# A tile of their own for the normalized rows, and a new order for the three products of split matmuls

## The chip, the core and the metric

The kernel runs on one core of a Trainium2 chip. The metric is the device time of one execution in microseconds (us), the median over runs. TensorE does the matmuls (PE in the rows, and PEld for its weight loads), VectorE is DVE, ScalarE is ACT, GpSimd is POOL, and SyncE (SP) issues the DMAs.

## What is computed

Eight batches of 3136 rows of 256 numbers go through a spectral filter and then through an MLP with a Fourier mix. Cut to what matters:

```python
# spectral filter
X = rfft(x, axis=1)
Yr = Xr @ w_r - Xi @ w_i + b_r ;  Yi = Xr @ w_i + Xi @ w_r + b_i
Y = softshrink(Yr, 0.01) + 1j * softshrink(Yi, 0.01)
x = irfft(Y, n=3136, axis=1)
# mix and MLP
u = x + real(fft(fft(x, axis=1), axis=2))
un = (u - mean(u)) / sqrt(var(u) + 1e-6)        # over the 256 numbers of a row
out = u + maximum(un @ w_ch1, 0) @ w_ch2        # 256 -> 1024 -> 256
```

## The kernel before

The Fourier transforms are matmuls against tables: 3136 is split into 64 by 49. Each batch b goes through stages, each of them a Python generator: `p1` (first transform, products into PSUM tile `g_f1`), `p2_f2` (second transform, `g_f2`, which yields X and the sums Xs), `p2_w` (the weights, `g_w`), `p2_mix` (the Fourier mix, `g_mix`, stored in DRAM as `md`), `p2_yt` and `p2_g2` (the way back, `g_yt` and `g_g2`, stored as `bd`), then the MLP in groups of three or four blocks of 128 rows: `p3_norm` loads `bf` and `mt` by DMA, multiplies (`g_g1`), adds `mt`, takes mean and variance and normalizes; `p3_tr` transposes the normalized rows on PE (`g_ut`); `p3_mlp1` multiplies with w1 into `h` and splits the rectified result; `p3_mlp2` multiplies with w2 into `o`, adds the rows and stores them.

To keep precision an operand is split in a high part and a low part (`hh` and `hl`, `uth` and `utl`, `bh` and `bl`, `xh` and `xl`, `Xh` and `Xl`, `yh` and `yl`). ACT makes the high part by a copy into the type fp32r; DVE (`lo_v`, L144, and L738 for `hl`) or POOL (`lo_g`, L147) then makes the low part as the difference. `mm3` multiplies two split operands by three matmuls into the same PSUM region: L150 is high left with low right, L151 low left with high right, L152 high with high. The left one is the stationary operand, for which a weight load goes ahead of every matmul. The operand that has just been made is the left one in `p3_mlp2` (`hh`, `hl`), and the right one in all the others (`p1`, `p2_w`, `p2_g2`, `p3_norm`, `p3_mlp1`), where the left one is a table or a weight.

Every `yield` gives a due time, and a heap runs the generators in that order, which gives the order in which instructions are traced. The tile context is opened with `schedule_with_timeline_sim=True`: a planner then orders the instructions of each engine by its own model of time, and takes a later one that is ready before an earlier one that is not. It also writes the semaphore waits: an instruction carries one, and further ones stand before it as separate EVENT_SEMAPHORE instructions on its queue. All DMAs are issued in order from the one queue of SP.

Tiles with the same tag share that tag's buffers in turn. Tag `mt` (2 KB per partition, 2 buffers) holds the rows loaded from `md` (L673, L675); L683 adds them to `g_g1` into `ut`; then L700 writes the normalized rows into the same `mt`, and L718 transposes them from there. It also holds scratch tiles while the weights are converted (`split_double`, L169 to L189), `wi` and `inv_f`. Tag `im` (0.8 KB, 2 buffers) is scratch in `p2_f2` between a copy on ACT (L445) and an add on DVE (L446), for the pieces that take the second branch: two of four in each quarter of batch 0, one of four in the others.

Of the kernel before, what the change touches and what calls it, by code (L numbers as in the profile page):

```python
# [10 lines left out]
F32 = mybir.dt.float32  # L11
# [117 lines left out]
def spectral_block(ctx: ExitStack, tc: tile.TileContext, x, w_ri, b_ri, w1, w2,  # L129
# [19 lines left out]
    def mm3(o, lh, ll, rh, rl, start=True, stop=True):  # L149
        te.matmul(o, lh, rl, start=start, stop=False)  # L150
        te.matmul(o, ll, rh, start=False, stop=False)  # L151
        return te.matmul(o, lh, rh, start=False, stop=stop)  # L152
# [5 lines left out]
    def split_double(name, h, l, sl, src):  # L158
# [3 lines left out]
        def tmp(tag, bufs, dt=I32):  # L162
            return sb.tile([128, 512], dt, tag=tag, bufs=bufs, name=f"cv_{name}_{tag}")
# [4 lines left out]
        tf = tmp("mt", 2, F32)  # L168
# [10 lines left out]
        r = tmp("mt", 2)  # L179
# [25 lines left out]
    def load_consts():  # L205
# [6 lines left out]
        wi = sb.tile([128, 2, D], F32, tag="mt", bufs=2, name="wi")  # L212
# [17 lines left out]
        inv = sb.tile([128, 128], F32, tag="mt", bufs=2, name="inv_f")  # L230
# [159 lines left out]
    def p2_f2(b):  # L390


        for q in range(4):
# [17 lines left out]
            for ui in range(4):  # L411
# [30 lines left out]
                else:  # L442
                    im = sb.tile([128, 2, 2, S], F32, tag="im", bufs=2, name="im")
# [178 lines left out]
    def p2_g2(b):  # L622

        bd = b_dram[b] = dr.tile([N2, 2, U, D], F32, tag="bd", bufs=4, name=f"bd{b}")
        for q in range(4):
            base, STEP, F2W, W0, WW, M0 = clock2(b, q)
            for i in range(4):
# [4 lines left out]
                for v in range(2):  # L632
                    cols = slice(v * D, v * D + D)
                    t = 2 * (i % 2) + v
                    if b == 0:
                        te.matmul(g[:98, cols], tih[:, t], yh[:, cols], start=True, stop=True)
                    else:
                        mm3(g[:98, cols], tih[:, t], til[:, t], yh[:, cols], yl[:, cols])
# [15 lines left out]
    def p3_norm(b):  # L654

        for gi, (g0, z) in enumerate(groups[b % 2]):
            t0, T3 = clock3(b, g0)
            for i, n in parts_of[z]:
# [8 lines left out]
                mt = sb.tile([128, 2, D], F32, tag="mt", bufs=2, name="mt")  # L667
# [30 lines left out]
                gp.tensor_mul(rs[:, :n], rs[:, :n], vv[:, :n])  # L698
                for j in range(n):
                    va.tensor_scalar(mt[:, j], ut[:, j], ag[:, j, 0:1], rs[:, j], op0=ALU.subtract, op1=ALU.mult)  # L700
                normed[b, gi, i] = mt
                uts[b, gi, i] = ut

    def p3_tr(b):
        for gi, (g0, z) in enumerate(groups[b % 2]):
            t0, T3 = clock3(b, g0)
            for i, n in parts_of[z]:
# [5 lines left out]
                mt = normed.pop((b, gi, i))  # L713
                g = gtile("g_ut")
                gv = g.rearrange("p (k t) -> p k t", k=2)
                for j in range(n):
                    for k in range(2):
                        te.transpose(gv[:, k, j * 128:(j + 1) * 128], mt[:, j, k * 128:(k + 1) * 128], ident)  # L718
# [4 lines left out]
    def p3_mlp1(b):  # L723
        for gi, (g0, z) in enumerate(groups[b % 2]):
            t0, T3 = clock3(b, g0)
            w = z * 128
            for f in range(8):
# [5 lines left out]
                for k in range(2):  # L733
                    mm3(h[:, :w], w1h[:, k, fs], w1l[:, k, fs], uth[:, k, :w], utl[:, k, :w], start=(k == 0), stop=(k == 1))
# [6 lines left out]
    def p3_mlp2(b):  # L741
        for gi, (g0, z) in enumerate(groups[b % 2]):
            t0, T3 = clock3(b, g0)
            for f in range(8):
# [5 lines left out]
                for j in range(z):  # L750
# [3 lines left out]
                        stop=(f == 7 and (j % 2 == 1 or j == z - 1)))  # L754
# [68 lines left out]
```

## Time and profile before

| | us |
|---|---|
| median of 3 runs (1953.55 to 1960.75) | 1956.1 |
| the profiled execution | 1961.45 |
| its span, first to last instruction | 1959.7 |
| around the span | 1.75 |
| PE busy in the span | 1856.2 |
| mean granted TensorE clock | 0.969 of full speed |

A row of a group of instructions names line, engine, operation, out<-in by the tiles' names and how often it ran, then busy time and mean duration, then the idle time of the engine just before them and what ended it. Matmuls overlap in the pipeline, so the distance between two starts, not the duration, is what one costs. Clock 1.00 is 2.4 GHz, and its lower level is 1.2 GHz.

### The profile page before, as it was taken

The page shows a single profiled execution, that of the slowest core. Times are in us where ns is not written, and L with a number is a line of the kernel's source. Part 1 is how long each engine was busy: PE and PEld are TensorE (multiplying, and loading weights), DVE is VectorE, ACT ScalarE, POOL GpSimd, SP SyncE. Part 2 cuts the span into 40 slices and gives each one's busy share as a digit, 9 for nine tenths or more (in the row PEclk, how much of TensorE's full clock was granted, in tenths as well). Part 3 has the DMA queues.
Part 4 walks back from the last instruction along what each step waited for, and adds up shares of the span by engine and source line. Part 5 has one row for each costly group of instructions (what it writes and reads, how often), then busy time and mean ns, then how long its engine had stood idle before and what let it go on. Part 6 is the DMA issues. An engine that isn't in the chain of part 4 may idle for free.

```text
span 1959.7 us, 35047 instructions
## 1 busy us (share of the span) xinstructions
PE 1856.2 (95%) x12115; PEld 1709.1 (87%) x12115; DVE 1322.5 (67%) x2831; ACT 853.2 (44%) x1888; POOL 704.8 (36%) x1087
## 2 busy tenths in 40 slices
PE   4875799999999999999999999999999999999999
PEld 3764699989999999998999999998999998998999
DVE  2676677777776777766677777766777766675543
ACT  2443544444444454443444544434544434433322
POOL 0345544344433444343333443323543322322210
PEclk7886899999999999999999999999999999999999
DMA  7466654345443544434443444435433332223210
GB/s 215 122 177 192 154 139 131 101 119 148 115 122 109 152 129 121 117 98 138 136 134 104 136 137 114 127 99 141 136 106 98 107 98 89 83 70 109 68 41 25
DMA packets 163540, 233.05 MB, mean 119 GB/s; under 512 B 27484, under 2 KB 107428, under 8 KB 163364
## 3 DMA queue, kind: packets, MB, share of 16 engines
q1 hardware_dynamic: 163364, 230.82, 41.9%
q8 instruction: 97, 1.59, 0.3%
q14 instruction: 79, 0.65, 0.1%
HBM read 127.95 MB, written 102.76 MB: 118 GB/s over the span
## 4 chain that ended last, share of the span: by engine, by line
PE 80%; DVE 7%; DMA 6%; SPq 3%; issue 2%; ACT 1%; POOL 1%; DVEq 0%; POOLq 0%; ACTq 0%
PE o L150 8%; PE o L151 8%; PE o L152 8%; PE h L150 8%; PE h L151 8%; PE h L152 8%; PE g_f L419 4%; PE g_w L150 3%; PE g_w L152 3%; PE g_w L151 3%; PE g_g L150 2%; PE g_g L152 2%; PE g_g L151 2%; PE g_yt L609 2%; PE g_ut L718 2%
## 5 line engine op out<-in xcount | busy, mean ns | idle before, releaser
L151 PE MATMUL o<-w2h,hl 128*128 128x256 f32 x1568 | 431.4, 285 | 8.4 <-DVE hl L738 8.4
L738 DVE SCALAR_TENSOR_TENSOR hl<-h,hh 128x512 fp32r<-128x512 f32 (+1 forms) x416 | 272.3, 655 | 243.8 <-ACT hh L737 242.5
L737 ACT ACTIVATE hh<-h 128x512 fp32r<-128x512 f32 (+1 forms) x416 | 238.0, 573 | 443.0 <-PE h L152 382.7
L152 PE MATMUL o<-w2h,hh 128*128 128x256 f32 x1568 | 424.2, 280 | 0.0
L150 PE MATMUL o<-w2l,hh 128*128 128x256 f32 x1568 | 397.6, 286 | 2.5 <-DVE ut L757 2.3
L150 PE MATMUL h<-utl,w1h 128*128 128x512 f32 (+1 forms) x832 | 323.5, 389 | 8.1 <-DVE hl L738 8.1
L152 PE MATMUL h<-uth,w1h 128*128 128x512 f32 (+1 forms) x832 | 317.0, 381 | 0.0
L151 PE MATMUL h<-uth,w1l 128*128 128x512 f32 (+1 forms) x832 | 316.6, 381 | 0.0
L151 PEld LDWEIGHTS o<-w2h,hl 128*128 128x128 f32 x1568 | 297.3, 190 | 14.8 <-DVE hl L738 10.3
L152 PEld LDWEIGHTS o<-w2h,hh 128*128 128x128 f32 x1568 | 297.0, 189 | 3.2
L150 PEld LDWEIGHTS o<-w2l,hh 128*128 128x128 f32 x1568 | 286.3, 189 | 15.1 <-ACT Xsh L428 2.9
L147 POOL TENSOR_TENSOR bl<-bf,bh 128x512 fp32r<-128x512 f32 x104 | 130.0, 1251 | 298.3 <-ACT bh L678 296.1
L419 PE MATMUL g_f<-tff,af 98*128 98x100 f32 x1024 | 155.2, 284 | 25.8 <-DMA tff<-c_tf 13.0
L419 PEld LDWEIGHTS g_f<-tff,af 98*128 98x128 f32 x1024 | 148.5, 204 | 34.2 <-issue 23.4
L152 PEld LDWEIGHTS h<-uth,w1h 128*128 128x128 f32 x832 | 156.8, 189 | 23.8
L150 PEld LDWEIGHTS h<-utl,w1h 128*128 128x128 f32 x832 | 157.0, 189 | 22.8 <-DVE hl L738 9.0
L147 POOL TENSOR_TENSOR xl<-xf,xh 128x512 fp32r<-128x512 f32 (+1 forms) x75 | 97.1, 1295 | 203.2 <-ACT xh L362 201.3
L151 PEld LDWEIGHTS h<-uth,w1l 128*128 128x128 f32 x832 | 157.3, 189 | 13.4
L683 DVE TENSOR_TENSOR ut<-g_g,mt 128x512 f32<-128x512 f32 x104 | 68.3, 657 | 104.9 <-PE g_g L152 67.9
L147 POOL TENSOR_TENSOR Xl<-xx,Xh 128x400 fp32r<-128x400 f32 (+1 forms) x96 | 106.3, 1110 | 89.6 <-ACT Xh L428 69.3
L147 POOL TENSOR_TENSOR Xsl<-xs,Xsh 128x200 fp32r<-128x200 f32 x120 | 76.9, 642 | 161.4 <-ACT Xsh L428 144.2
L700 DVE TENSOR_SCALAR mt<-ut,ag,rs 128x256 f32<-128x256 f32 x196 | 90.8, 502 | 48.9 <-POOL rs L698 48.6
(155 smaller groups left out, 3811.3 us busy)
## 6 DMA issues: line engine op xcount, KB each, us to landing
bd<-bev SPq DMA_DIRECT2D x128, 196.0 KB
af<-ad SPq DMA_DIRECT2D x62, 392.0 KB
bf<-bd SPq DMA_DIRECT2D x184, 128.0 KB
out_dram<-ut SPq DMA_DIRECT2D x92, 256.0 KB
xf<-in_x SPq DMA_DIRECT2D x176, 128.0 KB
ad<-ev SPq DMA_DIRECT2D x168, 128.0 KB
md<-mq SPq DMA_DIRECT2D x112, 192.0 KB
mt<-md SPq DMA_DIRECT2D x416, 32.0 KB
```

Source lines behind the costliest of these rows:

```text
L147: gp.tensor_sub(out_, full, hi.bitcast(F32))
L150: te.matmul(o, lh, rl, start=start, stop=False)
L151: te.matmul(o, ll, rh, start=False, stop=False)
L152: return te.matmul(o, lh, rh, start=False, stop=stop)
L419: te.matmul(g[:, o:o + 100], afs[s][:, ui * D + k * 128:ui * D + k * 128 + 128], tfs[s][:, ui], start=True, stop=True)
L609: te.transpose(gt[:100, (v * 2 + o) * 128:(v * 2 + o + 1) * 128], y[:, o, place].rearrange("p c j -> p (c j)"), ident)
L683: va.tensor_add(ut[:, :n], g[:, :w].rearrange("p (n d) -> p n d", d=D), mt[:, :n])
L700: va.tensor_scalar(mt[:, j], ut[:, j], ag[:, j, 0:1], rs[:, j], op0=ALU.subtract, op1=ALU.mult)
L718: te.transpose(gv[:, k, j * 128:(j + 1) * 128], mt[:, j, k * 128:(k + 1) * 128], ident)
L737: sc.activation(hh[:, :w], h[:, :w], AF.Relu)
L738: va.scalar_tensor_tensor(hl[:, :w], h[:, :w], 0.0, hh[:, :w].bitcast(F32), op0=ALU.max, op1=ALU.subtract)
```

## The change

`mm3` gets a parameter `first` that says which of the three products goes first; the other two follow in the order high·high, high·low, low·high. By default (`p1`, `p2_w`, `p3_norm`) the first is now high·high. In `p2_g2` and `p3_mlp1` it is high left with low right, as before, but the second and third change places. In `p3_mlp2` low left with high right, `hl`·w2h, is first. In all of them two products with the same stationary operand now follow each other. The normalized rows get a tile `nm` of the tag `mt`, which has three buffers instead of two; the tag `im` has one instead of two.

```diff
--- before.py
+++ after.py
@@ -146,10 +146,12 @@
     def lo_g(out_, full, hi):
         gp.tensor_sub(out_, full, hi.bitcast(F32))
 
-    def mm3(o, lh, ll, rh, rl, start=True, stop=True):
-        te.matmul(o, lh, rl, start=start, stop=False)
-        te.matmul(o, ll, rh, start=False, stop=False)
-        return te.matmul(o, lh, rh, start=False, stop=stop)
+    def mm3(o, lh, ll, rh, rl, start=True, stop=True, first=0):
+
+        ops = [(lh, rh), (lh, rl), (ll, rh)]
+        ops.insert(0, ops.pop(first))
+        for i, (l, r) in enumerate(ops):
+            te.matmul(o, l, r, start=start and i == 0, stop=stop and i == 2)
 
     UTB = 6
     st_eng = nc.sync
@@ -165,7 +167,7 @@
         raw = sb.tile([128, 1024], I32, tag="uth", bufs=2, name="raw_" + name)
         behind(1, out=raw.rearrange("p (f e) -> p f e", f=src.shape[1]), in_=src)
         lo, hi = raw[:, 0::2], raw[:, 1::2]
-        tf = tmp("mt", 2, F32)
+        tf = tmp("mt", 3, F32)
         sc.activation(tf, hi.bitcast(F32), AF.Abs)
         va.tensor_scalar(tf, tf, HI_MIN, HI_MAX, op0=ALU.max, op1=ALU.min)
         t = tf.bitcast(I32)
@@ -176,7 +178,7 @@
         wf = w.bitcast(F32)
         e = tmp("ut", UTB)
         va.tensor_scalar(e, w, -0x800000, None, op0=ALU.bitwise_and)
-        r = tmp("mt", 2)
+        r = tmp("mt", 3)
         va.tensor_scalar(r, lo, 8, None, op0=ALU.logical_shift_right)
         rf = tmp("ut", UTB, F32)
         va.scalar_tensor_tensor(rf, r, 2.0 ** -44, e.bitcast(F32), op0=ALU.mult, op1=ALU.mult)
@@ -209,7 +211,7 @@
         for name, tag in (("wr", "hh"), ("ws", "hh"), ("wd", "hl")):
             KF[name] = sb.tile([128, 2, D], F32, tag=tag, bufs=2, name=name + "f")
         behind("x", out=KF["wr"], in_=w_v[0])
-        wi = sb.tile([128, 2, D], F32, tag="mt", bufs=2, name="wi")
+        wi = sb.tile([128, 2, D], F32, tag="mt", bufs=3, name="wi")
         behind("x", out=wi, in_=w_v[1])
 
         for name, sign in (("ws", -1.0), ("wd", 1.0)):
@@ -227,7 +229,7 @@
         sc.copy(cs[:, :, 0], t[:, :, 0:128])
         lo_v(cs[:, :, 1], t[:, :, 0:128], cs[:, :, 0])
         sc.copy(cs[:, 0, 1, 0:1], t[:, 0, 128:129])
-        inv = sb.tile([128, 128], F32, tag="mt", bufs=2, name="inv_f")
+        inv = sb.tile([128, 128], F32, tag="mt", bufs=3, name="inv_f")
         nc.sync.dma_start(out=inv, in_=c_inv)
         split("inv", inv)
 
@@ -440,7 +442,7 @@
                     put(lo_g, [Xl, Xh], xv_)
                     va.tensor_add(xs, xx[:, :, :, 0], xx[:, :, :, 1])
                 else:
-                    im = sb.tile([128, 2, 2, S], F32, tag="im", bufs=2, name="im")
+                    im = sb.tile([128, 2, 2, S], F32, tag="im", bufs=1, name="im")
                     put(sc.copy, [Xh], gv)
                     sc.copy(im, gv[:, :, :, S:])
                     va.tensor_add(xs, gv[:, :, :, :S], im)
@@ -635,7 +637,7 @@
                     if b == 0:
                         te.matmul(g[:98, cols], tih[:, t], yh[:, cols], start=True, stop=True)
                     else:
-                        mm3(g[:98, cols], tih[:, t], til[:, t], yh[:, cols], yl[:, cols])
+                        mm3(g[:98, cols], tih[:, t], til[:, t], yh[:, cols], yl[:, cols], first=1)
                 bev = sb.tile([98, 512], F32, tag="bev", bufs=2, name="bev")
                 (va.tensor_copy if b else sc.copy)(bev, g[:98])
                 u = 8 * q + 2 * i
@@ -664,7 +666,7 @@
 
                 src = [(b - 1, m), (b, m)] if joint else [(b, m), (b, NM + m)]
                 bf = sb.tile([128, 512], F32, tag="bf", bufs=2, name="bf")
-                mt = sb.tile([128, 2, D], F32, tag="mt", bufs=2, name="mt")
+                mt = sb.tile([128, 2, D], F32, tag="mt", bufs=3, name="mt")
                 for r, (bb, n2) in enumerate(src):
                     nc.sync.dma_start(out=bf[r * 64:r * 64 + 64, :w].rearrange("p (n d) -> p n d", d=D),
                                       in_=n2_rows(b_dram[bb], n2, n))
@@ -696,9 +698,10 @@
                 gp.tensor_mul(vv[:, :n], vv[:, :n], rs[:, :n])
                 gp.tensor_scalar(vv[:, :n], vv[:, :n], -0.5, 1.5, op0=ALU.mult, op1=ALU.add)
                 gp.tensor_mul(rs[:, :n], rs[:, :n], vv[:, :n])
+                nm = sb.tile([128, 2, D], F32, tag="mt", bufs=3, name="nm")
                 for j in range(n):
-                    va.tensor_scalar(mt[:, j], ut[:, j], ag[:, j, 0:1], rs[:, j], op0=ALU.subtract, op1=ALU.mult)
-                normed[b, gi, i] = mt
+                    va.tensor_scalar(nm[:, j], ut[:, j], ag[:, j, 0:1], rs[:, j], op0=ALU.subtract, op1=ALU.mult)
+                normed[b, gi, i] = nm
                 uts[b, gi, i] = ut
 
     def p3_tr(b):
@@ -710,12 +713,12 @@
                     uth = sb.tile([128, 2, 512], F32R, tag="uth", bufs=2, name="uth")
                     utl = sb.tile([128, 2, 512], F32R, tag="utl", bufs=2, name="utl")
                     uthl[b, gi] = uth, utl
-                mt = normed.pop((b, gi, i))
+                nm = normed.pop((b, gi, i))
                 g = gtile("g_ut")
                 gv = g.rearrange("p (k t) -> p k t", k=2)
                 for j in range(n):
                     for k in range(2):
-                        te.transpose(gv[:, k, j * 128:(j + 1) * 128], mt[:, j, k * 128:(k + 1) * 128], ident)
+                        te.transpose(gv[:, k, j * 128:(j + 1) * 128], nm[:, j, k * 128:(k + 1) * 128], ident)
                 tw = slice(i * 128, i * 128 + n * 128)
                 sc.copy(uth[:, :, tw], gv[:, :, :n * 128])
                 lo_v(utl[:, :, tw], gv[:, :, :n * 128], uth[:, :, tw])
@@ -731,7 +734,7 @@
                 h = ps.tile([128, 512], F32, tag="h", bufs=2, name="h")
                 fs = slice(f * 128, f * 128 + 128)
                 for k in range(2):
-                    mm3(h[:, :w], w1h[:, k, fs], w1l[:, k, fs], uth[:, k, :w], utl[:, k, :w], start=(k == 0), stop=(k == 1))
+                    mm3(h[:, :w], w1h[:, k, fs], w1l[:, k, fs], uth[:, k, :w], utl[:, k, :w], start=(k == 0), stop=(k == 1), first=1)
                 hh = sb.tile([128, 512], F32R, tag="hh", bufs=2, name="hh")
                 hl = sb.tile([128, 512], F32R, tag="hl", bufs=2, name="hl")
                 sc.activation(hh[:, :w], h[:, :w], AF.Relu)
@@ -751,7 +754,7 @@
                     o = ops[j // 2][:, (j % 2) * D:(j % 2) * D + D]
                     js = slice(j * 128, j * 128 + 128)
                     mm3(o, hh[:, js], hl[:, js], w2h[:, f], w2l[:, f], start=(f == 0 and j % 2 == 0),
-                        stop=(f == 7 and (j % 2 == 1 or j == z - 1)))
+                        stop=(f == 7 and (j % 2 == 1 or j == z - 1)), first=2)
             for (i, n), o in zip(parts_of[z], ops):
                 ut = uts.pop((b, gi, i))
                 va.tensor_add(ut[:, :n], o[:, :n * D].rearrange("p (n d) -> p n d", d=D), ut[:, :n])
```

## Rows read from the trace of the kernel before

**Rows 1.** The page's part 1: the span, then busy time, share of the span and instructions of two engines.
```profile
span 1959.7 us, 35047 instructions
...
PE 1856.2 (95%) x12115; PEld 1709.1 (87%) x12115; DVE 1322.5 (67%) x2831; ACT 853.2 (44%) x1888; POOL 704.8 (36%) x1087
```

**Rows 2.** Busy time by stretch: length, then busy us and number of instructions of PE, PEld, DVE, ACT and POOL, then the granted clock, the busy share of the DMA engines and GB/s.
```profile
0.00:265.00 265.00, 186.35 (x895) 154.08 (x896) 157.38 (x307) 109.14 (x258) 98.03 (x126) 0.80 0.60 168
265.00:1955.00 1690.00, 1669.51 (x11221) 1554.88 (x11220) 1164.14 (x2524) 744.04 (x1632) 606.74 (x961) 1.00 0.40 111
1955.00:1960.00 5.00, 0.30 (x3) 0.10 (x1) 1.02 (x2) 0.00 (x0) 0.00 (x0) 0.71 0.23 80
```

**Rows 3.** What PE waited for from 250 us on, all of it: us in total, times, the longest.
```profile
PE o L151 <- DVE hl L738: 8.4, 10, 2.8
PE h L150 <- DVE hl L738: 8.1, 2, 4.8
PE o L150 <- DVE ut L757: 2.3, 2, 1.4
PE g_ut L718 <- DVE mt L700: 1.2, 3, 0.7
PE g_yt L609 <- DVE ut L683: 0.3, 1, 0.3
```

**Rows 4.** The same for the first 265 us, the longest, and those for POOL's low parts.
```profile
PE g_f L419 <- DMA tff<-c_tf: 13.0, 3, 9.4
PE g_f L419 <- DMA af<-ad: 12.2, 2, 8.5
PE g_ut L718 <- DVE mt L700: 12.0, 1, 12.0
...
PE g_g L150 <- POOL bl L147: 7.3, 1, 7.3
PE g_f L150 <- POOL xl L147: 5.6, 2, 3.2
```

**Rows 5.** Matmuls of PE in order of time, deep in the steady part: start, duration, engine, line, operation.
```profile
1014.43 0.28 PE L150 MATMUL o<-w2l,hh 128*128 128x256 f32 x1
1014.55 0.28 PE L151 MATMUL o<-w2h,hl 128*128 128x256 f32 x1
1014.66 0.28 PE L152 MATMUL o<-w2h,hh 128*128 128x256 f32 x1
1014.77 0.39 PE L150 MATMUL h<-utl,w1h 128*128 128x512 f32 x1
1015.00 0.40 PE L151 MATMUL h<-uth,w1l 128*128 128x512 f32 x1
```

**Rows 6.** First-transform matmuls of batch 0, which all have the same stationary operand, and their weight loads (groups by line: busy us, mean ns, idle before).
```profile
L313 PE MATMUL g_f<-xf,fwd 128*128 128x512 f32 (+1 forms) x26 | 13.1, 652 | 8.3 <-DMA xf<-in_x 8.3
L313 PEld LDWEIGHTS g_f<-xf,fwd 128*128 128x128 f32 x26 | 5.3, 214 | 15.7 <-issue 14.1 <-DVE ev L317 1.4 <-DMA xf<-in_x 0.2
```

**Rows 7.** The instructions of L718, the transposes: count, duration in ns (least/median/most), first and last start. The second row is its separate waits on PE's queue.
```profile
L718 PE MATMUL g_ut<-ident,mt x392: 270/272/445, 208.6 to 1921.8; 128*128 128x128 f32 x196
L718 PEldq EVENT_SEMAPHORE  x342: 51/51/6617, 200.4 to 1919.2; - x171
```

**Rows 8.** What the queue of SP waited for, two of its rows: us in total, times, the longest.
```profile
SPq L673 <- PE g_ut L718: 137.6, 54, 6.0
...
SPq L673 <- DVE mt L700: 45.1, 21, 6.0
```

**Rows 9.** PE in order of time: two `o` products of one line together, then three `h` products, then the next `o` products.
```profile
1004.79 0.48 PE L150 MATMUL o<-w2l,hh 128*128 128x256 f32 x2
1005.11 0.39 PE L150 MATMUL h<-utl,w1h 128*128 128x512 f32 x1
1005.34 0.39 PE L151 MATMUL h<-uth,w1l 128*128 128x512 f32 x1
1005.57 0.40 PE L152 MATMUL h<-uth,w1h 128*128 128x512 f32 x1
1005.81 0.28 PE L151 MATMUL o<-w2h,hl 128*128 128x256 f32 x1
```

**Rows 10.** The instructions of L738, which makes `hl`: count, duration in ns (least/median/most), first and last start.
```profile
L738 DVE SCALAR_TENSOR_TENSOR hl<-h,hh x416: 517/684/694, 228.2 to 1953.6; 128x512 fp32r<-128x512 f32 x107, 128x384 fp32r<-128x384 f32 x32
```

**Rows 11.** DVE in order of time around the longest wait of the steady part; in brackets the idle time before, and what ended it.
```profile
1343.46 0.69 DVE L683 TENSOR_TENSOR ut<-g_g,mt 128x512 f32<-128x512 f32 x1 [6.03 <-DMA mt<-md]
...
1346.00 0.69 DVE L738 SCALAR_TENSOR_TENSOR hl<-h,hh 128x512 fp32r<-128x512 f32 x1 [0.32 <-ACT hh L737]
```

**Rows 12.** PE in order of time at the same place.
```profile
1346.75 0.79 PE L150 MATMUL h<-utl,w1h 128*128 128x512 f32 x1 [4.75 <-DVE hl L738]
1347.34 0.63 PE L151 MATMUL h<-uth,w1l 128*128 128x512 f32 x1
```

**Rows 13.** The copy into `im` on ACT and the add that reads it on DVE: count, duration in ns (least/median/most), first and last start.
```profile
L445 ACT COPY im<-g_f x36: 328/342/359, 37.8 to 1691.9; 128x200 f32<-128x200 f32 x36
L446 DVE TENSOR_TENSOR xs<-g_f,im x36: 353/367/369, 38.3 to 1692.3; 128x200 f32<-128x200 f32 x36
```

**Rows 14.** What ACT waited for in the first 270 us, two of the rows: us in total, times, the longest. The first is for the scratch tile with which the weights' conversion begins.
```profile
ACT cv_w_mt L169 <- DMA raw_w<-in_w: 3.0, 2, 2.4
ACT Xh L432 <- DVE xs L446: 2.8, 3, 1.5
```

## The prediction

> **What bounds the kernel now.** I read the page's first part, then busy time by stretch, then PE's waits with the time at which they fall. In the page [rows 1] the reader should see that PE is the only engine near its limit: 1856.2 us of 1959.7. The stretches [rows 2] split this in two. From 265 to 1955 us PE is busy for 1669.51 of 1690 us, so only 20.5 us are idle, at full clock. In the first 265 us it is busy for 186.35, so 78.65 us are idle, at clock 0.80. Behind the last matmul lie 4.7 us of evictions and stores. So an edit pays in three ways only: PE does less, one of the few waits goes, or the beginning is shorter.
>
> The change leaves every matmul in place: the same products with the same shapes. What it can reach in the steady part is thus at most the 20.5 us. The list of waits there [rows 3] is complete (8.4 + 8.1 + 2.3 + 1.2 + 0.3 = 20.3 us), and 16.5 us of it are waits for `hl` from L738 on DVE. None is for POOL, and one small one of 1.2 us is for the normalized rows. In the beginning [rows 4] the long waits are for DMA and for the first normalization; 12.9 us in three waits are for low parts made by POOL (`bl`, `xl`).
>
> **The tile `nm`.** Today the transposes read a tile that DMAs have written, and L718 has 342 separate waits on PE's queue, of 51 ns each in the median [rows 7]: 17.4 us if each of them stood in PE's way. But PE's whole idle time before L718 in the steady part is 1.2 us [rows 3], ended by DVE: the waits pass while PE works off what it has. So the gain lies between 0 and 17.4 us, near the idle row: I take -0.5. The 12.0 us wait in the beginning [rows 4] is for the first normalization itself and stays. Is there a new wait? `mt` and `nm` take turns over three buffers. The `nm` of one part gets the buffer that the `mt` of the part before left at L683, earlier on the same engine. The `mt` of a part gets that of the `nm` two parts back, when its transposes are done: the same release as with two buffers today. So the 137.6 us for which SP's queue stands at L673 until transposes are done [rows 8] stay, with the six DMAs of each part and whatever is queued behind them (loads of `bf` and `xf`, stores): 0.
>
> **High·high first (`p1`, `p2_w`, `p3_norm`).** PE waits for ACT's high part alone, issues one product, and then waits for POOL. What is gained is one product of cover per wait. A 512-column product costs 0.23 us between starts [rows 5], about twice that at the lower clock. Three waits [rows 4] make 3 x 0.46 = 1.4 us at most, 0 at least; in the steady part there is no such wait to shorten. I take -0.5, since in the beginning PE meets another wait next.
>
> **`hl`·w2h first in `p3_mlp2`.** Today two high·low products can start before `hl` is there, and the planner uses that: it pulls two of them together, then three `h` products, and then goes on with `hl` [rows 9]. With `hl` first, the whole group stands behind it. Of 416 groups [rows 10] PE waited measurably at `hl` for 10, on average 0.84 us [rows 3]. If those waits lose the cover of two products (2 x 0.115 us, [rows 5]), that costs 10 x 0.23 = 2.3 us. If on the other hand the planner now puts the group later, as it must when nothing of it can go before `hl`, the gain is at most the 8.4 us. Three `h` products are 0.69 us, and waits shorter than that would go. I take -2. `h`'s own wait for `hl` (8.1 us in two waits) is another matter: there [rows 11] DVE stood 6.03 us at L683 for a DMA of `mt`, with `hl` queued behind it, and PE stood 4.75 us [rows 12] and restarted at the lower clock, 0.59 us from one product to the next where 0.23 is usual. The change doesn't make that DMA earlier: 0, with -10 as the end if the planner happens to place L683 later.
>
> The page "TensorE: Matmul & The Clock Gate" of the Trainium skill (section "Part 2: What happens when you issue a matmul") says that only weight loads are pulled ahead and matmuls stay in program order. That speaks against putting the latest operand first, since ready products can't pass it. The trace agrees so far as PE stands idle at `hl` instead of passing on. By that rule alone the term would be +2.3, by the planner's answer up to -8.4.
>
> **The exchange of second and third product** in `p3_mlp1` and `p2_g2`: the first, which waits for the low part, is the same, and the high part has long been there. 0.
>
> **`im` with one buffer.** A second copy on ACT (L445) must now wait for the add on DVE (L446, 0.367 us, [rows 13]). Two such pieces follow each other only in the four quarters of batch 0. At one add each that is 1.5 us, at the longest wait of ACT for L446 so far (1.5 us, [rows 14]) 6 us, and behind ACT stand the copies that free PSUM. PE mostly waits for DMAs there [rows 4]: I take +0.5, and 0 to 6 for the range. In other batches there is one piece per quarter: 0.
>
> **Three `mt` buffers in the weights' conversion.** ACT waited there for the DMA of the raw weights [rows 14], and no row has it wait for a buffer: 0, at best -2.
>
> **The planner's new order.** Other products and tiles give it another timeline, and it may shift every engine's order. No row shows this. The nearest are the 20.5 us of idle time in the steady part and the 78.65 us before. Half of the first and a tenth of the second would be some 10 and 8 us, in either direction. I take 0.
>
> **Sum:** -0.5 - 0.5 - 2 + 0.5 = -2.5 us. Against the profiled execution (1959.7 us of span and 1.75 around it, 1961.45) this is about 1959.0. The median of the runs lies 5.35 us lower, at 1956.1, so I predict 1953.6 us. What a measurement of this kernel can tell from no change is about 0.5%, 9.8 us, and the forecast lies well inside it, with 1945 to 1962 as its own range.
>
> **Rivals.**
> - *The waits for `hl` go.* With whole groups behind `hl`, the planner leaves DVE more time, both for `o` and `h`: all 16.5 us vanish, with some 2 us of slow restarts. 1956.1 - 18.5 = 1938. For it: these are the only waits of weight in the steady part [rows 3]. Against it: half of them come from a late DMA [rows 11, 12]. Chance 0.22.
> - *`hl` first blocks PE.* PE's queue holds back the two ready products and everything behind them, `h` products included, and those are what DVE and ACT need next. It decides when PE arrives before `hl` in more groups than now. At 10 of 416 it costs 2.3 us; at 30, each with 0.84 + 0.23 us, 32 - 8.4 = +24, so 1980; by 18 waits it passes 9.8 us. For it: L738 takes 0.684 us [rows 10] behind other work of a busy DVE. Against it: today's arrivals are mostly late enough. Chance 0.12. The loss of the `im` buffer and an unlucky order in the beginning add 0.04 on this side.
> - *It doesn't do what it says.* `nm` shares its tag with `mt`, so its buffers are still written by DMAs, only earlier, and the separate waits might remain. Then that term is 0 instead of -0.5, and the time about 1954. Chance 0.1, within no change.
> - *Weight loads fall away.* Two products with the same stationary operand are now neighbours in some 3190 triples. If the second load were left out, PE could at best go at one column per clock: 256 columns at 2.4 GHz are 0.107 us, where 0.115 is seen [rows 5], an estimate of 0.008 x 3190 = 25 us, so 1931. Against it: 26 neighbouring matmuls with one stationary operand had 26 loads [rows 6], and 512 columns take just twice the time of 256 [rows 5], so the load isn't what paces. Chance 0.03. The same page and section of the Trainium skill say that weights are loaded apart so that one load may serve many matmuls, which is this rival; the rows here don't bear it out.
>
> **Chances and range.** The forecast holds 0.49, and with "doesn't do what it says" no change has 0.59 in all, less some 0.02 for its lower edge: 0.57. Faster by over 0.5%: 0.22 + 0.03 + 0.02 = 0.27. Slower: 0.12 + 0.04 = 0.16. The range of 1936 to 1970 takes in the first rival, the planner's shifts and the ends of the small terms, and leaves out the blocking and the loads, with the edges some 0.2.
>
> **What would show it.** L718's separate waits should fall from 342 to a few with PE's idle time before L718 little changed; the wait for `bl` should move to the second product. PE's idle time between 265 and 1955 us should be 15 to 22 us, with `o`'s wait now on the first product. Matmul distances stay at 0.115 and 0.23 us, loads equal matmuls in number. I am wrong if idle time there falls under 10 or rises over 30 us, or if the first 265 us change by over 8.

## The result, and the profile after

| | median | lowest to highest | profiled execution | its span |
|---|---|---|---|---|
| before | 1957.3 us (5 runs) | 1953.55 to 1962.02 | 1961.45 us | 1959.7 us |
| after | 1976.46 us (5 runs) | 1970.72 to 1978.64 | 1970.72 us | 1968.6 us |

The changed kernel is slower: ratio 1.0092, 95% interval [1.0066, 1.0117], some 18 us. The forecast was 1953.6 us, the range ended at 1970. The profiled execution of after was the fastest of its five, and that of before 4 us above its median, so the two traces show less of the loss (9 us) than the medians do.

The page's part 1 of after (span, then busy time, share and instructions):

```profile
span 1968.6 us, 34589 instructions
...
PE 1863.1 (95%) x12115; PEld 1710.1 (87%) x12115; DVE 1341.5 (68%) x2831; ACT 851.0 (43%) x1888; POOL 708.2 (36%) x1087
```

Its busy time by stretch, with the columns of [rows 2]:

```profile
0.00:265.00 265.00, 187.37 (x926) 154.19 (x927) 159.02 (x315) 111.70 (x263) 104.58 (x128) 0.83 0.61 170
265.00:1955.00 1690.00, 1666.15 (x11124) 1546.74 (x11123) 1179.24 (x2511) 737.30 (x1621) 603.64 (x960) 1.00 0.39 111
1955.00:1969.00 14.00, 9.62 (x68) 9.21 (x67) 3.25 (x6) 1.97 (x4) 0.00 (x0) 0.99 0.08 28
```

Read the middle stretch against [rows 2]. PE is idle for 23.85 us there, 3.36 more than before; yet in nearly the same busy time it gets through 97 products fewer (11124 against 11221). Of these 31 now stand in the first stretch, as the MLP starts earlier, and 65 in the last. So most of the loss isn't waiting: the products themselves follow each other more slowly. The instructions that make `hl` (count, duration, first and last start; compare [rows 10]) mark the same stretch by its ends:

```profile
L741 DVE SCALAR_TENSOR_TENSOR hl<-h,hh x416: 519/681/694, 222.9 to 1962.8; 128x512 fp32r<-128x512 f32 x107, 128x384 fp32r<-128x384 f32 x32
```

From the first to the last there are 1739.9 us, where before had 1725.4 [rows 10]: the MLP starts 5.3 us earlier and then loses 14.5 us. Which products? In the start times of all matmuls, `o` (256 columns) goes from 116.3 to 118.8 ns from one start to the next, while `h` (512 columns) stays at 230.3 and 230.7. These are means over the products that run at full clock and have no transpose or other unsplit fp32 product next to them; for `o` some 4,300 to 4,500 of 4,704. Twenty-four `o` products of after in a row, the first two and the last two (PE in order of time):

```profile
1817.77 0.28 PE L154 MATMUL o<-w2h,hl 128*128 128x256 f32 x1
1817.88 0.28 PE L154 MATMUL o<-w2h,hh 128*128 128x256 f32 x1
...
1820.38 0.28 PE L154 MATMUL o<-w2h,hh 128*128 128x256 f32 x1
1820.50 0.28 PE L154 MATMUL o<-w2l,hh 128*128 128x256 f32 x1
```

2.73 us over 23 distances are 118.7 ns. 2.5 ns more for 4,704 products are 11.8 us. With the 3.36 us of idle time that makes 15.2 us, where 14.5 are to be explained. PE's waits from 265 us on are spread otherwise than in [rows 3], with little more in all:

```profile
PE o L154 <- DVE hl L741: 8.3, 8, 1.6
PE g_ut L721 <- DVE nm L703: 4.3, 7, 0.8
PE g_f L154 <- DVE yl L144: 3.7, 2, 1.9
PE h L154 <- DVE hl L741: 3.0, 3, 1.7
PE o L154 <- DVE ut L760: 2.4, 2, 1.2
```

The transposes' separate waits, to compare with [rows 7]:

```profile
L721 PEldq EVENT_SEMAPHORE  x41: 51/51/51, 203.3 to 1860.2; - x41
```

SP's wait for the transposes, to compare with the first row of [rows 8]:

```profile
SPq L675 <- PE g_ut L721: 2.2, 1, 2.2
```

All waits of SP's queue together barely fell, from 1031 to 1016 us: the queue now stands elsewhere, for example at the stores of `mq` (before, then after):

```profile
SPq L565 <- DVE mq L559: 52.5, 17, 14.9
...
SPq L567 <- DVE mq L561: 95.5, 21, 14.9
```

### The profile page after: what moved, and what is told of

It reads as the page before. It is cut to its first block, busy times and chain, and to the rows that moved or that the text cites. A ratio compares the mean times of both kernels' runs of the same rounds, so it can differ in the third digit from the quotient of the medians.

```text
span 1968.6 us, 34589 instructions
## 1 busy us (share of the span) xinstructions
PE 1863.1 (95%) x12115; PEld 1710.1 (87%) x12115; DVE 1341.5 (68%) x2831; ACT 851.0 (43%) x1888; POOL 708.2 (36%) x1087
## 4 chain that ended last, share of the span: by engine, by line
PE 76%; DVE 10%; DMA 6%; SPq 3%; POOL 2%; issue 2%; ACT 1%; DVEq 0%; POOLq 0%; ACTq 0%
PE o L154 24%; PE h L154 22%; PE g_w L154 10%; PE g_g L154 6%; PE g_f L421 4%; PE g_yt L611 2%; PE g_f L154 2%; PE g_ut L721 2%; PE g_mix L543 1%; DVE nm L703 1%; DVE eo L521 1%; DVE hl L741 1%; DMA md<-mq 1%; DMA xf<-in_x 1%; DMA mt<-md 1%
## 5 line engine op out<-in xcount | busy, mean ns | idle before, releaser
L154 PE MATMUL o<-w2h,hl 128*128 128x256 f32 x1568 | 452.0, 288 | 10.8 <-DVE hl L741 8.3
L154 PE MATMUL o<-w2l,hh 128*128 128x256 f32 x1568 | 441.7, 282 | 0.0
L154 PE MATMUL o<-w2h,hh 128*128 128x256 f32 x1568 | 441.6, 282 | 0.0
L154 PEld LDWEIGHTS o<-w2h,hl 128*128 128x128 f32 x1568 | 296.1, 189 | 22.9 <-DVE hl L741 11.8
L154 PEld LDWEIGHTS o<-w2l,hh 128*128 128x128 f32 x1568 | 296.7, 189 | 0.2
L703 DVE TENSOR_SCALAR nm<-ut,ag,rs 128x256 f32<-128x256 f32 x196 | 105.0, 575 | 45.3 <-POOL rs L700 43.6
```

The lines of the kernel that those rows point to most:

```text
L154: te.matmul(o, l, r, start=start and i == 0, stop=stop and i == 2)
L703: va.tensor_scalar(nm[:, j], ut[:, j], ag[:, j, 0:1], rs[:, j], op0=ALU.subtract, op1=ALU.mult)
```

## The experiments

What could slow `o`? The change puts two products with the same `hh` side by side (theory A). It also moves tiles: a third `mt` buffer (2048 bytes) and one `im` buffer fewer (800 bytes) shift everything behind them in SBUF, `w2h` and `w2l` by 1248 bytes (theory B). Or the planner's new layout does it (theory C). The traces carry no addresses; the places named below are those of the program's allocation.

**One part at a time.** The order alone: `mm3` with `first=` as in the diff, tiles as before.

> The kernel before with the new order of the three products alone; the tiles mt, im and the normalised rows stay as they were, so every tile lies at its old address. The changed kernel took 0.9% (about 18 us) more than before, and its trace gives most of that to the 256-column products o of the second MLP product: 118.8 ns from start to start against 116.3 ns, over 4704 of them 11.7 us; another 11 us went into longer idle stretches of TensorE. Theory A (the order hl, hh, hh, where the same hh block is loaded twice in a row, costs the 2.5 ns): o at about 118.8 ns, time about 1967 to 1975 us. Theory B (w2's halves moved by 1248 bytes in SBUF when mt got a third buffer and im lost one, and reading them there costs the 2.5 ns): o at about 116.3 ns, time within 1950 to 1962 us. Theory C (no single part: the planner lays out all engines' work anew for any edit): anything, and o follows neither part.

The tiles alone: `nm`, three `mt` buffers, one `im` buffer, `mm3` as before.

> The kernel before with the new tiles alone: the normalised rows in a tile of their own under mt's tag, three mt buffers, one im buffer; the three products in their old order. Theory A (order costs the 2.5 ns for each o): o at about 116.3 ns, time 1948 to 1960 us, with the first product of the MLP about 5 us earlier as in the changed kernel. Theory B (the place of w2 in SBUF): o at about 118.8 ns, time about 1963 to 1977 us. Theory C (the planner's new layout): anything.

The changed kernel with one product back in its order:

```
-  mm3(o, hh[:, js], hl[:, js], w2h[:, f], w2l[:, f], ..., first=2)
+  te.matmul(o, hh[:, js], w2l[:, f], start=st, stop=False)      # st, sp: start and stop as before
+  te.matmul(o, hl[:, js], w2h[:, f], start=False, stop=False)
+  te.matmul(o, hh[:, js], w2h[:, f], start=False, stop=sp)
```

> The changed kernel, with the second MLP product alone back in its old order (hh with w2's low half, hl with its high half, hh with its high half). Theory A: o falls back to 116.3 ns and about 11.7 us of the 18 us come back: about 1960 to 1966 us. Theory B: o stays at 118.8 ns, time 1966 to 1978 us. Theory C: o between, time anything within 10 us of the changed kernel.

And a mere nudge of the planner: `NRM` from -1.239 to -1.235.

> The kernel before with nothing changed but the due time of the normalisation, from -1.239 to -1.235 of a group's time: the planner lays some work out in another order, every instruction and address stays. It measures how far such a reshuffle alone moves the time. Theories A and B: within 0.3% of before (1951 to 1963 us), o at 116.3 ns. Theory C: it may move by as much as the change did, 0.5 to 1%.

| run | `o`, ns | median, us | ratio to before |
|---|---|---|---|
| order alone | 116.4 | 1966.17 | 1.0032 [1.0018, 1.0047] |
| tiles alone | 118.7 | 1975.82 | 1.0077 [1.0063, 1.0090] |
| changed, old second product | 118.9 | 1971.55 | 1.0063 [1.0046, 1.0079] |
| nudge | 116.3 | 1962.76 | 1.0016 [1.0004, 1.0027] |

Each ratio here and below is to runs of the kernel before made beside the run: their median was 1960.56 us for these four, 1956.79 for the next four, 1956.03 and 1958.51 for the two groups of the last table. So ratios compare between tables, medians don't.

Theory A falls: `o`'s distance goes with the tiles, whatever the order. The order has a price of its own of 0.3%, more than theory B had allowed for the order alone (1962 us at most), and the nudge shows that half of that can come from a reshuffle. Where the first expectation speaks of another 11 us of idle stretches, the stretches above show 3.36 us. The tiles alone cost more than the changed kernel without its new second product; that is taken up below.

**Is it `w2`'s place?** The kernel before with `w2` cut into padded tiles:

```
+  p = sb.tile([128, 2 * D + 40], F32R, tag=f"W{k}_{q}", bufs=1, ...)   # four for w2h, four for w2l
```

> The kernel before (old order, old tiles) with w2's halves cut into four tiles of two f blocks each, every tile padded by 160 bytes, so that the eight tiles lie at 32, 64, 96, 0, 32, 64, 96 and 0 bytes beyond a multiple of 128 (the whole halves lay at 32 in the kernel before and at 0 in the changed one). The distance of o's products is then read for each tile in one run. Theory B as far as the first four runs bear it out (old addresses 116.3 ns, new addresses 118.7 ns, whatever the order): the distance follows the tile's place, so tiles at 0 show about 118.7 ns and tiles at 32 about 116.3 ns, with time between 1956 and 1968 us. Rival B2 (not w2's place but that of another tile that moved with mt and im): all eight show 116.3 ns, time 1955 to 1963 us. Rival B3 (the place matters on a coarser grid than 128 bytes): tiles with the same remainder differ from one another.

The changed kernel with 32 empty bytes ahead of `w2h`, and the kernel before with 1248:

```
-  h = sb.tile(shape, F32R, tag=f"W{2 * i}", bufs=1, name=name + "h")
+  h = sb.tile([128, 8 * D + 8], F32R, tag="W2", bufs=1, name="w2h")[:, 8:].rearrange(...)
```

> The changed kernel with w2's high half, and all tiles behind it, 32 bytes further on, so that both halves lie at 32 bytes beyond a multiple of 128, as in the kernel before. Theory B: o back at 116.3 ns, about 11 us less than the changed kernel: 1960 to 1967 us. Rival B2 (another tile's place): o stays at 118.8 ns, 1971 to 1978 us. Rival B3 (a coarser grid): o anywhere.

> The kernel before with w2's halves, and the tiles behind them, moved by 1248 bytes, to the addresses that they have in the changed kernel (the high half keeps its tile's start and leaves 1248 bytes empty); order, buffers and all other addresses stay. Theory B: o at 118.7 ns and 11 us more than before: 1968 to 1974 us. Rival B2: o at 116.3 ns, time within 1955 to 1964 us.

The new order in the second product alone, on the kernel before:

> The kernel before with the new order in the second MLP product alone (hl with w2's high half, hh with its high half, hh with its low half); the other split products and the tiles stay. The order alone cost 0.3% (6 us) over all products, and TensorE's waits for hl in o rose from 8.4 to 14.7 us in that run. If that rise is the cost (hl first blocks TensorE's queue where hl comes late): 1963 to 1968 us, o's waits for hl 12 to 16 us. If the cost came from the other products (high with high first): 1957 to 1962 us, o's waits for hl at about 8 us.

| run | `o`, ns | median, us | ratio to before |
|---|---|---|---|
| cut and padded | 118.6 | 1965.69 | 1.0044 [1.0027, 1.0062] |
| changed, `w2` + 32 bytes | 116.1 | 1964.21 | 1.0039 [1.0025, 1.0053] |
| before, `w2` + 1248 bytes | 118.8 | 1964.92 | 1.0049 [1.0034, 1.0064] |
| new second product alone | 116.2 | 1960.81 | 1.0026 [1.0010, 1.0041] |

32 bytes give back over half of the loss, and 1248 bytes alone cost 0.49% (forecast was 11 us and 1968 to 1974; `o` came out as forecast, the time 3 us below). Twenty-four `o` products of the kernel with 1248 bytes in a row, the first and the last, are 2.73 us apart, 118.7 ns each:

```profile
1839.43 0.28 PE L150 MATMUL o<-w2l,hh 128*128 128x256 f32 x1
...
1842.16 0.28 PE L152 MATMUL o<-w2h,hh 128*128 128x256 f32 x1
```

But the cut tiles don't fit theory B in the form put down for them: of the two tiles at 32 beyond a multiple of 128, the first of `w2h` showed 116.6 to 117.6 ns and the first of `w2l` 119.0 to 119.4. A tile's own remainder modulo 128 isn't what counts.

In the last run PE's waits for `hl` rose from 8.4 us in [rows 3] to 16.0 us; with the order alone, second row, to 14.7:

```profile
PE o L754 <- DVE hl L738: 16.0, 15, 2.4
PE o L154 <- DVE hl L740: 14.7, 14, 2.1
```

The waits are those forecast if this rise is the price; the time (1960.81 us) is that of the other branch, so the run doesn't decide between them. In the changed kernel itself the same waits are 8.3 us at 8 places, as the list above shows: there the rise is absent.

**TensorE alone.** Two kernels of their own measure the distance with no other engine at work:

```
a = st[:, so + j * 128:so + j * 128 + 128]               # stationary; so in steps of 8 elements, 32 bytes
rh, rl = mv[:, mo:mo + n], mv[:, mo + far:mo + far + n]  # moving; mo in steps of 8 elements
te.matmul(o[:, :n], a, rl, start=j == 0, stop=False)     # then low*high and high*high
```

> A kernel of its own that leaves out the whole computation: TensorE alone works through triples of split products on tiles of zeros, with no other engine busy beside it. In blocks of 24 products of 256 columns the moving operand is moved on in steps of 32 bytes over 1024 bytes, then the stationary operand, then the distance between the two moving halves; then the same with 512 columns. The theory that w2's own place sets the distance of o's products (116.3 or 118.7 ns, as the kernels with old and new addresses showed, whatever the order) expects blocks of 256 columns to differ by 2 to 3 ns with the place of one operand or with the offset between the two. If all blocks show one distance to within 0.5 ns, the place of TensorE's operands by itself costs nothing, and the 2.5 ns come from what other engines or transfers do in SBUF at the same time.

> Again a kernel of its own that leaves out the whole computation: triples of split products on zeros, TensorE alone. The run before showed, with no other engine busy, distances from 113.5 to 120.0 ns for 256 columns and 226.7 to 234.1 ns for 512, the same at every place 256 bytes further on. This one goes through all 64 pairs of remainders (moving, stationary) in steps of 32 bytes modulo 256, for 256 columns in the old and the new order, and for 512, 400 and 384 columns. The theory that the pair of places alone sets the distance expects, for the pair of the kernel before (w2 at 160, hh and hl at 224) 116.3 ns, for that of the changed kernel (128 and 224) 118.7 ns, within 0.5 ns, in both orders; for h's pair (224 and 224 with 512 columns) about 230.3 ns; and at the pair (64, 128) 113.5 ns. A rival, that something else moved with w2, expects no such agreement.

The first shows 113.5 to 120.0 ns for 256 columns; the same figures come back every 256 bytes, to 0.5 ns. The second, in order of time, shows 26 products of nearly one pair each (two belong to a neighbouring block): moving operand at 128 and stationary at 192 modulo 256, then 128 and 224 (the changed kernel's pair), and the latter again in the new order:

```profile
182.18 3.14 PE L158 MATMUL oo<-mv,st 128*128 128x256 f32 x26
184.93 3.28 PE L158 MATMUL oo<-mv,st 128*128 128x256 f32 x26
366.75 3.28 PE L158 MATMUL on<-mv,st 128*128 128x256 f32 x26
```

Less the last product's own 0.28 us, 25 distances make 114.4, 120.0 and 120.0 ns: the place counts, the order doesn't. Three forecasts missed: the old and the new pair show 117.8 and 120.1 ns, 2.3 apart where the kernels have 2.4 to 2.6, but both some 1.4 higher; the pair (64, 128), which gave 113.5 in the first of these kernels, gave 117.8 here; and `h`'s pair (224, 224) gave 226.7 ns with 512 columns, not 230.3. Sorted by the difference of the two places, moving less stationary, modulo 256, the 64 blocks of 256 columns fall into order:

| difference | 0 | 32 | 64 | 96 | 128 | 160 | 192 | 224 |
|---|---|---|---|---|---|---|---|---|
| most of the eight pairs, ns | 119.5 to 119.7 | 117.7 to 117.9 | 117.7 to 117.9 | 119.7 to 120.0 | 118.4 to 118.6 | 117.2 to 117.4 | 117.7 to 117.8 | 118.4 |
| those that stand apart | 120.0, 120.2 | 116.9 (two) | | | 119.9 | 120.1 (two) | 113.9, 114.0 | 118.1, 118.2 |

At a difference of 192 the distance is 113.9 or 117.8, at 160 it is 117.2 or 120.1, and nothing between. `w2` and `hh` lay 192 apart (160 and 224) in the kernel before and 160 apart (128 and 224) in the changed one.

**Back in the kernel, by the map.** Eight runs: each starts from the kernel before or the changed one, with empty bytes ahead of `hh` (a tile that nothing uses), of `w2h`, or of both. The third also puts `hl`'s product last, the seventh is the kernel before unedited, and the last takes back the second product's order as well. The empty tile, here 64 bytes:

```
+  sb.tile([128, 16], F32, tag="pad", bufs=1, name="pad")
```

> The kernel before with 64 empty bytes ahead of hh: every tile from hh on moves by 64, so that hh and hl lie at remainder 32 and w2's halves at 224 modulo 256. Nothing else is edited. The map of TensorE alone gives 114.0 ns for this pair and 117.8 ns for that of the kernel before (160, 224): if the pair is what counts in the kernel, o falls by about 3.8 ns to 112 to 113 ns, over some 4,300 products in running stretches 16 us: 1938 to 1946 us, faster than either kernel. If what counts is another tile, or the map doesn't carry over to a kernel in which other products come between: o at 116 to 119 ns, 1953 to 1970 us.

> The changed kernel with 64 empty bytes ahead of hh and 32 more ahead of w2, so that hh and hl lie at 32 and w2's halves at 224 modulo 256, the same pair as in the kernel with the 64 bytes alone. The map gives 120.1 ns for the changed kernel's pair and 114.0 ns for this one: if the pair is what counts, o falls from 118.8 to about 113 ns, 26 us: 1944 to 1953 us, and what is left against the kernel before at this pair (about 6 us) is the price of the change's order and tiles. Otherwise 1962 to 1978 us.

> The kernel before with the 64 empty bytes, and in the second MLP product the order hh with w2's low half, hh with its high half, hl with its high half: hl, which VectorE writes last, is wanted last. The change put hl first; with that order alone TensorE's waits for hl in o rose from 8.4 to 16.0 us. If the wait is the price of the order: waits for hl at 3 to 7 us and a time 2 to 6 us below that of the 64 bytes alone, about 1934 to 1943 us. If the order's price lay in how the planner lays the rest out: within 3 us of the 64 bytes alone, or above it.

> The kernel before with w2's halves and the tiles behind them moved by 96 bytes, so that w2 lies at 0 modulo 256 and hh and hl stay at 224. The map gives 117.9 ns for this pair against 117.8 ns for the old one: if the pair is what counts, o stays at 116.3 ns and the time within 1952 to 1961 us, although w2 has moved and lies on a multiple of 128, as in the changed kernel. If it is any move, or the multiple of 128 by itself: o at 118.7 ns, 1964 to 1970 us.

> The kernel before with 224 empty bytes ahead of hh: w2's halves lie at 128 modulo 256, as in the changed kernel, but hh and hl at 192 where they lay at 224. With w2 at 128 and hh at 224 the kernel before showed 118.8 ns and 1965 us. If the place of w2 against hh and hl counts: o at 116.5 ns or less and 1952 to 1961 us. If w2's own remainder counts: o again at 118.8 ns, 1963 to 1968 us.

> The kernel before with 64 empty bytes ahead of hh and 192 ahead of w2: w2's halves stay at their old remainder of 160 modulo 256, hh and hl move to 32. If the place of w2 against hh and hl counts, as in the map (119.9 ns for this pair against 117.8 ns for the old one): o at 118 to 119 ns, 1963 to 1969 us. If w2's own remainder counts: o at 116.3 ns, 1953 to 1961 us.

> The kernel before, unedited, for its trace on the chip of this call. If the distances belong to the program: o at 116.3 ns and h at 230.3 ns, as in its first trace. If they belong to the chip or the run as well: o up to 117 ns and h up to 231.4 ns.

> The changed kernel with both suspects taken back and all else left in (the tiles, the order of the other split products): w2 32 bytes further on, at 160 modulo 256, and the second MLP product in its old order. If these two make up the loss: o at 116.3 ns and a time within 0.2% of before, 1953 to 1960 us. If a third part costs too: 1962 us and more.

| run | `w2`, `hh`: difference | `o`, ns | median, us | ratio to before |
|---|---|---|---|---|
| before again | 160, 224: 192 | 116.3 | 1959.16 (one run) | |
| before, "best" pair | 224, 32: 192 | 116.5 | 1958.11 | 1.0009 [0.9999, 1.0019] |
| the same, `hl` last | 224, 32: 192 | 116.6 | 1960.81 | 1.0031 [1.0018, 1.0044] |
| changed, "best" pair | 224, 32: 192 | 116.6 | 1969.92 | 1.0070 [1.0056, 1.0084] |
| before, all + 224 | 128, 192: 192 | 116.5 | 1959.49 | 1.0004 [0.9988, 1.0020] |
| changed, `w2` + 32, old second product | 160, 224: 192 | 116.4 | 1959.66 | 1.0005 [0.9992, 1.0018] |
| before, `w2` + 96 | 0, 224: 32 | 117.5 | 1961.70 | 1.0028 [1.0017, 1.0039] |
| before, `hh` moved | 160, 32: 128 | 118.9 | 1968.47 | 1.0042 [1.0027, 1.0057] |

The forecasts that took a pair for itself fell: at the map's "best" pairs `o` stands at 116.5, not 113 ns, nothing beats the kernel before, and `w2` 96 bytes on wasn't free. The difference fits them better, with the runs above: 116.1 to 116.6 ns at 192 in eleven traces, 117.5 at 32, 118.7 to 118.9 at 160 in four, 118.9 at 128. At 192 three different pairs show the same. At 32, 128 and 160 only one pair each was tried in the kernel (all four traces at 160 have 128 and 224), so there pair and difference aren't told apart. Nor does the map give the kernel's figures: at 160 six of its eight pairs have 117.2 to 117.4, lower than most at 192. So `w2` at 128, as in the changed kernel, costs nothing once `hh` lies at 192, and `w2` at its old 160 costs 0.42% once `hh` lies at 32. That the difference is the measure was read from these runs afterwards; it forecast none of them. The cut tiles, read again by it, bear out 192 and leave the rest open: they lie 192, 96, 0, 160, 64, 224, 128 and 32 from `hh`, and from start to next start the first shows 116.8 to 117.4 ns, the other seven 117.9 to 119.2.

With both suspects taken back, the changed kernel is as fast as before, its new tiles and the exchanged order of every other product still in it. Two runs stay aside. The changed kernel at the "best" pair has `o` at 116.6 ns and yet 1.0070, where 32 bytes alone gave 1.0039. Part of the other 0.3% may be the clock: its granted clock was 0.970 in the mean of its six executions, 0.972 for the kernel before beside it, which is some 9 us more at the lower level, at most some 4 us lost, an estimate from these means. And the tiles alone have the same distance as the kernel before with 1248 bytes, 118.7 ns, but 1.0077 against 1.0049; its clock was not lower than before's (0.973 against 0.971). What cost these two the other 0.3% isn't settled.

Why 116.5 ns, a figure that TensorE alone never showed at 192? Runs of 24 `o` products in the kernel with all moved by 224, the first and the last product of two of them:

```profile
1729.79 0.28 PE L150 MATMUL o<-w2l,hh 128*128 128x256 f32 x1
...
1732.50 0.28 PE L152 MATMUL o<-w2h,hh 128*128 128x256 f32 x1
...
1835.75 0.28 PE L150 MATMUL o<-w2l,hh 128*128 128x256 f32 x1
...
1838.37 0.28 PE L152 MATMUL o<-w2h,hh 128*128 128x256 f32 x1
```

2.71 and 2.62 us over 23 distances: 117.8 and 113.9 ns in one execution, the same two figures as with TensorE alone. The mean is a mixture. What sends a run to the one or the other isn't settled.

With `hl` last, PE's longest waits were these:

```profile
PE o L755 <- DVE ut L760: 8.4, 4, 4.2
PE o L757 <- DVE hl L739: 8.0, 7, 2.4
```

The waits for `hl` are back at 8 us, but another has come up at DVE, for the eviction that frees `o`'s PSUM tile, and against the same places with the old order the time rose by 0.2%. So `hl` last bought nothing, and 0.2% is about what the nudge alone did: these runs don't show where the order's price lies.

## Why the prediction was wrong

**The step that failed** is the list of parts itself. "Matmul distances stay at 0.115 and 0.23 us" was a premise without a term. The tiles were costed by who waits for their buffers; that their sizes move the tiles behind them was not asked. `o`'s distance rose by 2.5 ns, which over 4,704 products is 11.8 us; moving `w2` alone, with what lies behind it, measured 0.49%, 9.6 us. That is half of the loss, and larger than the whole sum of the forecast. The sign it had set for PE's idle time (wrong under 10 or over 30 us) didn't catch it: idle time was 23.85 us, and most of the loss lay in busy time.

**The planner's new order and `hl`·w2h first** (-2, bounds +2.3 and -8.4; planner 0, up to 18 either way): the new second product alone measured +0.26%, 5 us, with waits for `hl` at 15 places instead of 10 and 7.6 us more of them. The sign was wrong, and the bound of +2.3 was too tight: it lengthened today's waits and added none. With the new tiles these waits are no higher than before (8.3 us in the changed kernel and with `w2` 32 bytes on), and yet taking the new second product back gave 0.34% in the latter (1.0039 to 1.0005): where that price lies isn't shown. As the nudge moved the time by 0.16%, and `hl` last by 0.2%, how much of the 5 us belongs to this order and how much to any reshuffle stays open.

**`hl` first blocks PE** was the rival with the right sign. Its mechanism is seen in the two kernels with the new order and the old tiles, at a fifth of its price (14 and 15 waits, short of the 18 from which it was to decide), and not in the changed kernel (8 waits). So far as it got the sign right for the changed kernel, that was luck.

**`nm`** (-0.5): the separate waits fell from 342 to 41, and bought nothing that can be measured. SP's 137.6 us at L673, which were to "stay" because the buffers rotate as before, went with the new tiles (2.2 us are left at L675, 3.2 with the tiles alone, 137.0 with the order alone). That reading was wrong, and the price of 0 was right for another reason: the queue stood almost as long as before, at other places. Why the wait moved isn't shown. Tiles and order with `w2` back at 160 gave 1.0039, the order alone 1.0032, so there, but for the place, all the tiles together cost nothing that can be told apart.

**High·high first, the exchange, `im`, the weights' conversion** (together 0): the kernel that keeps them all and takes back the two suspects gave 1.0005 [0.9992, 1.0018]. PE's wait for `bl` did leave the list of the first 265 us, and one for ACT took its place:

```profile
PE g_g L154 <- ACT bh L680: 5.2, 1, 5.2
```

**The beginning** became 5.3 us shorter, less than the 8 that were to count against the forecast. It isn't a gain to explain: the kernel before, profiled again, started its MLP 3.1 us earlier than in its first profile.

**The sum now:** the order 0.32%, `w2`'s place 0.49%, the other tiles 0.07% make 0.88% of the 0.92% measured. Taken off the changed kernel step by step, the second product's order is 0.29% (to 1.0063), `w2`'s place 0.58% (to 1.0005), and 0.05% is left. Each ratio is uncertain by 0.10 to 0.26%, so the two sums agree. The tiles alone, with 0.77% where this sum has 0.49 + 0.07, are not explained by it.

## What to carry to other kernels

When an edit changes a tile's size or its number of buffers, list which other tiles change their address, and read the start-to-start distance of the commonest matmul in both traces before looking for waits: busy time and waits alone don't show it. A shift of 32 bytes gave back more here (0.53%) than any reordering. Where a kernel waits for 1% of its time, a new order of products can cost as much by reshuffling as it was to gain; a placebo nudge tells how much that is.

## What the runs showed of the hardware

With no other engine at work, 256-column products of this kind take 113.5 to 120.2 ns from start to start, and 512-column ones 226.6 to 234.1 ns, depending mostly on how far apart the moving and the stationary operand lie modulo 256 bytes. The Trainium skill, "TensorE: Matmul & The Clock Gate", section "Part 2: What happens when you issue a matmul", says that the two operands have independent read ports, so that loading the next weights takes no bandwidth from the running matmul. That gives no reason why the places of the two should matter to each other; here they do, and the measurement decides. Whether it is the load that gets in the way of the stream wasn't tried.

At one difference a run of products can keep either of two distances from beginning to end (113.9 or 117.8 ns at 192). And `h` rose by about 1 ns in five kernels in which its own operands had not moved against each other (231.2 to 231.4 against 230.3); that is not explained.
